# One SyncE queue, two weight loads moved behind two token-block transposes

## The chip, the cores and the metric

The kernel runs on one core of a Trainium2 chip. Its time is the device time of one execution in microseconds (us). Five engines work from instruction streams of their own: TensorE (PE, with its weight loads shown apart as PEld), VectorE (DVE), ScalarE (ACT), GpSimd (POOL) and SyncE (SP). SP computes nothing here: it issues every DMA of the kernel, in the order in which they stand in its stream. Three runs of the kernel before gave 298.45, 300.27 and 296.32 us, a median of 298.45 us.

## The reference

The program is one transformer block over 2048 tokens of width 640, in bf16. The first half normalises the tokens, projects them to Q, K and V, and runs attention of 32 heads of 20 channels in four segments of 512 tokens; each segment mixes a causal softmax attention of its own with a read from a memory that the segments before it have filled. The second half is a feed-forward layer of width 1728.

```python
for s in range(4):                       # segments of 512 tokens
    logits = einsum('bhqd,bhkd->bhqk', qs, ks) * scale + mask
    a_dot  = einsum('bhqk,bhkd->bhqd', softmax(logits), vs)
    num    = einsum('bhld,bhde->bhle', phi(qs), M)
    den    = einsum('bhld,bhd->bhl',  phi(qs), z)[..., None] + 1e-06
    outs.append(g * num / den + (1 - g) * a_dot)
    M = M + einsum('bhld,bhle->bhde', phi(ks), vs)
    z = z + phi(ks).sum(tokens)
h  = x + concat(outs) @ wo               # phi(t) = t+1 if t > 0 else exp(t)
h2 = h + silu(layernorm(h) @ w1) @ w2    # x is normalised before wq, wk, wv too
```

## The kernel before

Tokens are held in 16 blocks of 128. A segment is four blocks. For a segment the blocks are normalised (`layer_norm`: statistics on DVE, the reciprocal root on POOL, the subtraction and scaling on DVE into `xn_rot`, L772), and each normalised block is turned, so that channels lie on partitions, into a tile of `tT`. For blocks 0 to 3 TensorE does the turning; for all later ones SP issues a DMA transpose (L796). The name of that step is `n1_tr` and the block: `n1_tr8` to `n1_tr11` are the four blocks of segment 2. They read `xn_rot`, written by `n1_ap8` to `n1_ap11`.

TensorE then projects to Q and K (`pr`), V (`v`, from `wv_sb`), and works through the eight groups of four heads: scores (`qk`, L943), their exponentials on ACT (`e`, L964 or L960) with the causal mask on POOL (`mk`, L976), the product with V (`av`, L999), a turn back (`td`), and the division on DVE (`nm`). `mz` (L1117) adds a segment to the memory: 96 small matmuls for segment 0. The output of a segment goes through a transpose (`ot`, L1166), the output projection (`wo`, from `wo_sb`), a second normalisation, the feed-forward layer's first product (`h1`, from the five chunks of `w1_sb`), tanh and a multiply, and the second product (`h2`, from `w2_sb`). Work of one segment's attention is interleaved with the feed-forward work of the segment before.

What order the work has is written out by hand. One long list, `ORDER`, names every step, with the buffer slots that it takes and, behind a slash, its engine. A program walks over that list and appends each step to its engine's stream; waits on semaphores are put in where a step reads what another engine or a DMA writes. An engine does its steps strictly in list order, so a step that waits holds up all behind it on its engine.

The stretch of the list that the change touches lies in segment 1's attention. Weights that are used late are loaded there: `w_w1_0` to `w_w1_4` are five chunks of w1 (432 KB each), `w_wo` is all of Wo (800 KB), `w_w2_0` to `w_w2_5` are w2. They wait for the early weight loads to have been rearranged, which is long past here, and the first three chunks of w2 also wait for segment 0's Q and K, whose place they take. On SP the stretch reads, one after another: `w_w1_2`, `w_w2_0`, `kt04`, `n1_tr8`, `n1_tr11`, `w_w1_1`, `w_wo`, `n1_tr10`, `n1_tr9`, `w_w2_1`, `ot0`. The lines that record these are L586 (a weight load), L796 (a token transpose), L1106 (a transpose of the memory's keys, `kt`) and L1166 (`ot`).

Of the kernel before, what the change touches and what calls it, by code (L numbers as in the profile page):

```python
# [333 lines left out]
D = 640  # L334
# [54 lines left out]
mk6a mk6e mk6b qk7a0:4,2 e7a0:6 av5:6 e7a2 mk7a mz03:0 mz02 mz00 mz01 kt04:3 mz04 n1_tr8:1 ma0:0 n1_ap10:1 oe5/D:1  # L389
pr130.0:7 qk7b0:0,4 e7b0:0 e7b2 mk7b mzc1 pr130.1 qe130/D:0 pa130:0 v13.0:2 v13.1 ve13/D qk8a0:6,0 e8a0:1 td5:4 nm5:0  # L390
av6:5 oe6/D:0 pr140.0/C:2 e8a2 mk8a mb01:0 mzc0 mb00:0 ex101:0 av7:7 oe7/D:1 qk8b0:5,3 e8b0:6 e8b2 td6:0 nm6:3 pr140.1
qe140/D:0 td7:5 nm7:0 n1_tr11 w_w1_1 w_wo:0 n1_tr10 n1_tr9 qk8e0:6,0 e8e0:3 pr131.0:2 pa120:0 pr131.1 qe131/D pb101
pa131:0 e8e2 mzc4 mk8b mb02:0 qk9a0:6,3 e9a2:5 e9a0 pr121.0:5 pr121.1 qe121/D pa110:0 pr141.0:2 qk9b0:0,3 e9b0:0 e9b2
pr141.1/C qe141/D mk8e av8:5 oe8/D:0 w_w2_1 ot0:0 wo0.0/C:6 wo0.1/C rs0 n2_st0:2 n2_rs0 ex131:0 qk10a0:2,0 e10a0/W:2
ot1 wo1.0:4 wo1.1 rs1 n2_st1:7 ot2 wo2.0:6 ex120:1 qk10b0:0,2 e10b2/W:1 wo2.1 rs2 n2_ap0:1 pb120 ot3 wo3.0:4 wo3.1
# [932 lines left out]
```

## Time and profile before

| what | value |
|---|---|
| median of three runs, lowest, highest | 298.45, 296.32, 300.27 us |
| profiled execution, first to last instruction (the page gives its time as this span alone) | 298.8 us |
| PE busy | 282.4 us, 95% |
| DVE, ACT, POOL busy | 219.3, 216.6, 148.4 us |
| chain that ended last | PE 64%, ACT 16%, DVE 11%, issue 4%, DMA 2% |
| mean granted TensorE clock | 0.994 |

A row of a view of instructions in order of time gives the start, the time from the first to the last of the group's instructions, the engine, the source line, the operation, the tile written and the tiles read, and in brackets how long the engine had been idle and what ended that; "issue" means that the engine waited for nothing that the profile shows. A row of the view of stretches gives, for each engine, busy time and instruction count, then the granted clock, the busy share of the 16 DMA engines and the rate that they moved. In the view of DMA, queue q1 carries the transfers that SP issues; the two queues called "instruction" carry instructions to the engines.

### The profile page before, as it was taken

How to read it: one execution, taken by the hardware profiler on the slowest of the kernel's cores; microseconds unless marked ns; L12 is line 12 of the kernel's file. 1: busy time of each engine (PE TensorE's matmuls, PEld its weight loads, DVE VectorE, ACT ScalarE, POOL GpSimd, SP SyncE). 2: the span in 40 equal slices, each digit the busy share in tenths (PEclk: the TensorE clock that was granted, in tenths of full speed). 3: DMA queues.
4: the chain of work that ended last, by engine and by line, in shares of the span. 5: the costliest groups of instructions: out<-in, count | busy, mean ns of one | idle time of the engine just before them, and what ended most of it. 6: DMA issues, size and time to landing. Idle time of an engine off the chain costs nothing.

```text
span 298.8 us, 8471 instructions
## 1 busy us (share of the span) xinstructions
PE 282.4 (95%) x3537; PEld 158.5 (53%) x3561; DVE 219.3 (73%) x447; ACT 216.6 (72%) x263; POOL 148.4 (50%) x297
## 2 busy tenths in 40 slices
PE   7899889699999999999989899999999999999996
PEld 5554434345554454566643464466564557764574
DVE  4879899478999857889978958498664676733614
ACT  5899999589989999966889865979979741004500
POOL 4888786652787544955545652348554720300000
PEclk9999999989999999999999999999999999999999
DMA  7859359927430500353454321402331021320003
GB/s 223 283 183 201 54 126 220 207 75 114 82 77 1 121 2 3 57 104 59 47 134 123 63 48 29 80 2 40 75 68 46 2 53 39 66 76 14 0 2 110
DMA packets 48597, 24.72 MB, mean 83 GB/s; under 512 B 38896, under 2 KB 47472, under 8 KB 48560
## 3 DMA queue, kind: packets, MB, share of 16 engines
q1 hardware_dynamic: 48560, 24.19, 35.8%
q8 instruction: 28, 0.46, 0.7%
q14 instruction: 9, 0.07, 0.1%
HBM read 10.41 MB, written 2.62 MB: 44 GB/s over the span
## 4 chain that ended last, share of the span: by engine, by line
PE 64%; ACT 16%; DVE 11%; issue 4%; DMA 2%; POOL 2%; ACTq 0%; DVEq 0%
PE ps_all L550 46%; ACT PT L964 11%; PE ps_all L551 7%; PE ps_all L943 5%; PE ps_all L999 4%; DVE stt L754 3%; ACT PT L960 2%; DVE xn_rot L772 2%; DVE sT L1222 2%; DMA tT<-otok 2%; ACT th L1216 1%; POOL PT L976 1%; DVE x_tok L1181 1%; ACT ex L873 1%; PE ps_all L1117 1%
## 5 line engine op out<-in xcount | busy, mean ns | idle before, releaser
L964 ACT ACTIVATE PT<-ps_all 128x1024 bf16<-128x1024 f32 x114 | 109.3, 1035 | 18.9 <-PE ps_all L943 18.2
L976 POOL TENSOR_SCALAR_AFFINE_SELECT PT<-PT 128x512 bf16<-128x512 bf16 x128 | 82.0, 649 | 60.5 <-ACT PT L964 34.5
L1216 ACT ACTIVATE th<-ps_all 128x512 f32<-128x512 f32 (+1 forms) x56 | 31.6, 585 | 37.0 <-PE ps_all L550 28.1
L550 PE MATMUL ps_all<-w_sb,sT 128*128 128x320 bf16 x400 | 58.2, 299 | 0.1
L550 PE MATMUL ps_all<-tT,w_sb 128*128 128x512 bf16 x225 | 53.9, 379 | 1.7 <-DVE x_tok L1259 0.8
L1222 DVE SCALAR_TENSOR_TENSOR sT<-th,ps_all 128x512 bf16<-128x512 f32 (+1 forms) x56 | 36.2, 663 | 17.6 <-ACT th L1216 17.1
L550 PEld LDWEIGHTS ps_all<-w_sb,sT 128*128 128x128 bf16 x400 | 38.1, 98 | 16.6 <-issue 1.5
L960 ACT ACTIVATE PT<-ps_all 128x2048 bf16<-128x2048 f32 x23 | 43.2, 1879 | 3.4 <-PE ps_all L943 3.0
L550 PEld LDWEIGHTS ps_all<-tT,w_sb 128*128 128x128 bf16 x235 | 21.4, 98 | 25.4 <-issue 2.2
L754 DVE BATCH_NORM_STATS2 stt<-x_tok 128x6 f32<-128x320 bf16 x62 | 26.8, 474 | 1.2 <-DMA x_tok<-in_A_x_dram 1.1
L1259 DVE SCALAR_TENSOR_TENSOR x_tok<-ps_all,x_tok 128x640 bf16<-128x640 f32 (+1 forms) x17 | 13.2, 784 | 18.0 <-PE ps_all L550 17.1
L1077 POOL TENSOR_TENSOR otok<-on 128x320 bf16<-128x320 bf16 x24 | 19.2, 806 | 12.6 <-DVE on L1069 12.6
L867 DVE CAST QK<-ps_all 128x512 bf16<-128x512 f32 x26 | 17.9, 687 | 8.0 <-PE ps_all L550 6.5
L764 POOL TENSOR_TENSOR rst<-mvt,eps_c 128x1 f32<-128x1 f32 x32 | 7.0, 219 | 31.8 <-DVE mvt L757 30.0
L550 PE MATMUL ps_all<-tT,wkr 128*128 128x512 bf16 (+1 forms) x87 | 21.7, 368 | 0.7 <-issue 0.5
L550 PE MATMUL ps_all<-wv_sb,tT 128*128 128x320 bf16 x130 | 20.1, 303 | 2.3 <-issue 2.3
L550 PE MATMUL ps_all<-tT,wqr 128*128 128x512 bf16 (+1 forms) x79 | 20.0, 367 | 1.3 <-issue 0.6
L772 DVE TENSOR_SCALAR xn_rot<-x_tok,mvt,rst 128x640 bf16<-128x640 bf16 x32 | 17.8, 563 | 4.3 <-POOL rst L766 3.8
L1069 DVE TENSOR_TENSOR on<-ps_all,rd 128x640 bf16<-128x640 f32 x24 | 19.8, 824 | 0.8
L766 POOL TENSOR_TENSOR rst<-rst,eps_c 128x1 f32<-128x1 f32 x32 | 18.0, 563 | 2.5
L1015 DVE TENSOR_SCALAR oTs<-ps_all,lsc 128x512 bf16<-128x512 f32 x24 | 17.8, 742 | 1.7 <-PE ps_all L999 1.6
L999 PE MATMUL ps_all<-PT,Vx 128*32 128x512 bf16 (+3 forms) x384 | 17.3, 301 | 0.0
(113 smaller groups left out, 381.8 us busy)
## 6 DMA issues: line engine op xcount, KB each, us to landing
out_dram<-x_tok SPq DMA_DIRECT2D x15, 160.0 KB, 1.9
w_sb<-in_B_w_dram SPq DMA_DIRECT2D x5, 432.0 KB, 4.5
x_tok<-in_A_x_dram SPq DMA_DIRECT2D x3, 640.0 KB, 4.4
w_sb<-in_B_w_dram SPq DMA_DIRECT2D x3, 480.0 KB, 4.1
QKV<-QK SPq DMA_DIRECT2D x12, 72.0 KB
wv_sb<-in_A_wv_dram SPq DMA_DIRECT2D x1, 800.0 KB, 8.2
wo_sb<-in_A_wo_dram SPq DMA_DIRECT2D x1, 800.0 KB, 6.4
w_sb<-in_B_w_dram SPq DMA_DIRECT2D x1, 640.0 KB, 5.0
```

What stands on the lines that cost most here:

```text
L550: return [lambda e: e.matmul(out, lhsT=lhsT, rhs=rhs, start=start, stop=stop)]
L551: return [lambda e, p=p: e.matmul(out[p:p + 32, :], lhsT=lhsT[:, p:p + 32], rhs=rhs, start=start, stop=stop, tile_position=(0, p)) for p i ...
L754: T.add(DV, lambda e, hh=hh: e.bn_stats(out=stt[:, s, 6 * hh:6 * hh + 6], in_=xb[:, 320 * hh:320 * hh + 320]), reads=R((xa, xsub)), writes ...
L772: T.add(eng, lambda e: e.tensor_scalar(out=xn_rot[:, xn.slot, :], in0=x_tok[:, b % 12, :], scalar1=mvt[:, s, 0:1], scalar2=rst[:, s, :], o ...
L960: T.add(AC, lambda e: e.activation(out=o, in_=src, func=ACT.Exp, scale=SCALE), reads=[("ps", z.slot + q) for z in (a, b) for q in range(2) ...
L964: T.add(AC, lambda e: e.activation(out=pt[:, pta.slot, q0:q0 + 2, 0:width], in_=sc3[:, b0:b0 + 2, 0:width], func=ACT.Exp, scale=SCALE), re ...
L976: fns.append(lambda e, v=v: e.affine_select(out=v, in_=v, pattern=[[0, 4], [1, 128]], compare_op=ALU.is_ge, fill=0.0, base=0, channel_mult ...
L999: fns.append(lambda e, j=j, r=r, h=h, pa=pa, pt=pt, co=co, q0=q0, ji=ji: e.matmul(bank(po)[32 * r:32 * r + 32, q0:hi], lhsT=vtile(vx)[:, j ...
L1069: T.add(DV, lambda e: e.tensor_tensor(out=on[:, ona.slot, :, :].rearrange("p b (x e) -> p b x e", e=DH), in0=v[:, :, :, 0:DH], in1=r2.unsq ...
L1077: T.add(PO, lambda e: e.tensor_tensor(out=o_dst, in0=on[:, ona.slot, 0, :].rearrange("p (i x) -> p i x", i=4), in1=on[:, ona.slot, 1, :].r ...
L1216: T.add(AC, lambda e: e.activation(out=th[:, tha.slot, lo:hi], in_=bank(ps)[:, lo:hi], func=ACT.Tanh, scale=0.5), reads=R((ps, [0])), writ ...
L1222: T.add(DV, lambda e: e.scalar_tensor_tensor(out=sT[:, f, lo:hi], in0=th[:, tha.slot, lo:hi], scalar=1.0, in1=bank(ps)[:, lo:hi], op0=ALU. ...
```

## The change

Five names of the list are put in another order. `n1_tr9` and `n1_tr10` change places with each other and go in front of the loads of Wo and of w1's chunk 1, which change places with each other too.

```diff
-qe140/D:0 td7:5 nm7:0 n1_tr11 w_w1_1 w_wo:0 n1_tr10 n1_tr9 qk8e0:6,0 e8e0:3 pr131.0:2 pa120:0 pr131.1 qe131/D pb101
+qe140/D:0 td7:5 nm7:0 n1_tr11 n1_tr9 n1_tr10 w_wo:0 w_w1_1 qk8e0:6,0 e8e0:3 pr131.0:2 pa120:0 pr131.1 qe131/D pb101
```

All five are steps of SP. No instruction is added or removed, no other engine's stream changes its order, and every transfer has the size that it had.

## The prediction

> **What bounds the kernel now.** I began with the page: shares of the engines, the slices of time, the DMA queues, and the chain that ended last.
>
> ```profile
> span 298.8 us, 8471 instructions
> PE 282.4 (95%) x3537; PEld 158.5 (53%) x3561; DVE 219.3 (73%) x447; ACT 216.6 (72%) x263; POOL 148.4 (50%) x297
> q1 hardware_dynamic: 48560, 24.19, 35.8%
> q8 instruction: 28, 0.46, 0.7%
> PE 64%; ACT 16%; DVE 11%; issue 4%; DMA 2%; POOL 2%; ACTq 0%; DVEq 0%
> ```
>
> TensorE sets the end with nearly two thirds of the chain, and DMA waits are 2% of it. What deserves a look is the 4% of "issue", some 12 us in which the chain's engine waited for nothing visible. I went through the chain in order of time around the five moved steps, then took stretches there.
>
> ```profile
> core 0: us, PE busy (x) PEld busy (x) DVE busy (x) ACT busy (x) POOL busy (x), PEclk, DMA share, GB/s
> 50.60:55.84 5.24, 4.85 (x138) 2.48 (x137) 4.05 (x10) 4.86 (x6) 3.09 (x5) 1.00 0.91 275
> 55.84:58.17 2.33, 0.00 (x0) 0.00 (x0) 0.24 (x1) 0.64 (x1) 1.44 (x3) 1.00 1.10 103
> 58.17:62.20 4.03, 4.03 (x44) 1.79 (x48) 2.33 (x4) 2.35 (x3) 0.34 (x1) 0.58 0.55 147
> ```
>
> From 55.84 to 58.17 TensorE does nothing, the other engines run dry behind it, and afterwards the granted clock is 0.58 for 4.03 us. TensorE's own rows show that the hole lies inside one group of matmuls:
>
> ```profile
> 51.88 0.73 PE L999 MATMUL ps_all<-PT,sT 128*32 128x512 bf16 x16
> 52.47 0.94 PE L1117 MATMUL ps_all<-sT,phiKt 128*32 128x63 bf16 x96
> 54.86 0.98 PE L550 MATMUL ps_all<-wv_sb,tT 128*128 128x320 bf16 x6
> 58.17 1.08 PE L550 MATMUL ps_all<-wv_sb,tT 128*128 128x320 bf16 x4 [2.34 <-issue]
> 60.12 1.26 PE L999 MATMUL ps_all<-PT,sT 128*32 128x512 bf16 x16
> ```
>
> Ten matmuls of V's projection share operands that were there at 54.86; six run, four come 2.3 us late. No operand can be missing, so I looked for the instructions. Queue q8 moves 0.46 MB in 28 records, about 16.4 KB each, and PE and PEld have 3537 + 3561 = 7098 instructions: 253 to a record. So q8 is TensorE's instruction stream. Finding its records and counting what TensorE did between them gives:
>
> ```profile
> 31.90:42.75 10.85, 9.15 (x120) 4.52 (x120) 10.04 (x23) 10.85 (x13) 8.84 (x21) 1.00 0.40 92
> 42.75:55.70 12.95, 12.23 (x257) 5.86 (x256) 11.17 (x24) 12.49 (x15) 9.83 (x22) 1.00 0.83 228
> 42.75:51.75 9.00, 8.44 (x127) 3.62 (x125) 8.37 (x19) 8.93 (x11) 6.75 (x17) 1.00 0.78 191
> 55.70:61.05 5.35, 3.01 (x26) 1.20 (x28) 1.92 (x5) 1.97 (x3) 1.44 (x3) 0.75 0.89 151
> ```
>
> Records stood at 42.75, 55.70 and 61.05. Normally 240 instructions pass between two; here 513 passed, then 54. One block had been used up by about 51.75 (127 + 125 = 252), which is when the next was due; TensorE went on with the block that it still had, and that one is used up at 513: the stop. The 96 tiny matmuls at 52.47, with 96 weight loads, burn most of that block in one microsecond, so this block gives only 4.09 us of cover (51.75 to 55.84). What filled those 4 us on the DMA engines is SP's work:
>
> ```profile
> 47.93 2.62 SPq L796 DMA_TRANSPOSE tT<-xn_rot  x2
> 50.59 0.58 SPq L586 DMA_DIRECT2D w_sb<-in_B_w_dram  x1
> 51.21 0.43 SPq L586 DMA_DIRECT2D wo_sb<-in_A_wo_dram  x1
> 54.52 3.24 SPq L796 DMA_TRANSPOSE tT<-xn_rot  x2
> 57.81 0.58 SPq L586 DMA_DIRECT2D w_sb<-in_B_w_dram  x1
> 65.66 5.17 SPq L1166 DMA_TRANSPOSE sT<-otok  x4
> ```
>
> In half-microsecond stretches of the DMA view, q1 is full up to 55.5 and the instruction record comes in the next one:
>
> ```profile
> q1 hardware_dynamic: 154, 0.19, 104.7%
> q1 hardware_dynamic: 236, 0.11, 81.2%
> q8 instruction: 1, 0.02, 12.1%
> ```
>
> The first row is 55.0 to 55.5, the other two 55.5 to 56.0. The block was served when the queued w1 chunk and Wo were through. These are two of the loads that the change moves.
>
> **The change part by part.** It removes and adds nothing; only issue times and the traffic at 51.75 change. SP's order up to `n1_tr11` is the same, and so is all before 50.6 us.
>
> *The transposes.* Each waits for its normalised block:
>
> ```profile
> 50.77 0.43 DVE L772 TENSOR_SCALAR xn_rot<-x_tok,mvt,rst 128x640 bf16<-128x640 bf16 x1
> 53.83 0.66 DVE L772 TENSOR_SCALAR xn_rot<-x_tok,mvt,rst 128x640 bf16<-128x640 bf16 x1
> DMA to landing us min/median/max: 3.4/3.4/3.4
> 76.44 2.22 PE L550 MATMUL ps_all<-wv_sb,tT 128*128 128x320 bf16 x15
> ```
>
> `n1_tr9` can go at 51.20, when the first of these ends (0.6 us after SP is free), instead of about 55.8; `n1_tr10` at 54.5, as before. The landing row is `n1_tr9`'s of before: 55.8 + 3.4 = 59.2, and block 9 is read first at 76.44. It had 17 us to spare, so the earlier landing is worth nothing by itself.
>
> *The loads.* SP now stands at `n1_tr10` until 54.5, and behind that stand Wo and the w1 chunk. With 1.2 us of issue for the transpose (2.62 for two, above, is 1.3 each), Wo goes at about 55.8 instead of 51.2, the w1 chunk at 56.3 instead of 50.6, `w_w2_1` near 57 instead of 57.8.
>
> ```profile
> DMA to landing us min/median/max: 6.4/6.4/6.4
> 69.70 1.53 PE L551 MATMUL ps_all<-wo_sb,sT 128*32 128x320 bf16 x40
> L550 PE MATMUL ps_all<-tT,w_sb x25: 379/379/390, 88.4 to 97.7; 128*128 128x512 bf16 x25
> ```
>
> Wo took 6.4 us to land; from 55.8 that is 62.2, against 69.70 (or 66 with the hole gone). w1 is read from 88.4. Both are hidden; the cover is the 4 us between 62.2 and 66. The `ot` transposes, next on SP, wait for attention's output and are reached at about 62 then, not 65.66. Of the moved burst (800 + 432 + 480 KB with `w_w2_1`) 1712 KB are to be moved from about 57, and at 0.19 MB per half microsecond, the row above, that takes 4.5 us: through at 61.7. I charge nothing for it.
>
> *The instruction block.* Due at 51.75, it now finds one or two transposes in flight instead of 1232 KB of loads. Upper bound of the gain: the whole hole, 2.33, plus the slow clock. The clock's loss is at most 4.03 x (1 - 0.58) = 1.69; from single rows, the product with V took 1.26 against 0.73, so 0.53 is seen in that group alone. TensorE was busy 4.03 of 4.03 us there, so I take a value near the top, 1.5. Sum of the bounds: 0 to 4.0. Lower bound 0: the block comes as late as before. No trace row prices a block due between two transposes, so I bound its delay: with nothing in the way it would be under 1 us; with both transposes ahead of it, until about 53.6 to 54 (51.2 + 2.6, the issue time of two, as the scale). From record to first matmul it took 58.17 - 55.70 = 2.47 us, so a record by 53.4 leaves no hole and one at 54 leaves 0.6. I take 0.2 left.
>
> The engines all stood still together, so nothing had run ahead that could swallow the shift, and what follows hangs on TensorE's chain, not on fixed times. Sum: -2.33 - 1.5 + 0.2 = -3.6 us. Of the profiled 298.8 that leaves 295.2; the median of 298.45 stands 0.35 lower, so 294.9.
>
> [...]
>
> **The rivals.**
>
> *The loads are not what held the block (no change, 298.4).* TensorE may have stopped for something other than its instructions, the record may be late for its own reasons, or the DMA engines might serve q8 between q1's packets whatever is queued; then order in q1 is irrelevant and the hole stays. For: I infer the link from one coincidence in time and a second after 58, when the record of 61.05 also came at the end of a load. Against: both came just then, and 513 less 252 is one block. [...] The full q1 ahead of the record disagrees so far.
>
> *The hole only shrinks (about 296.7).* Transposes hold the block to about 54.5; the hole is 1.1 us, without the low clock or with half of it. Gain 1.2 from the hole and some 0.6 of clock: 1.8.
>
> *The hole moves (299.2, slower).* The next block is due when TensorE enters the last one, about 55.8, exactly where the moved burst now starts. Served first or between, it costs nothing. Served last, it decides by the end of the burst: the 114 + 119 instructions from 58.17 to 69.00 show that the block in hand lasts until about 65.4 once 3.6 us are gone. At the 7.0 us in which 1232 KB went before (50.6 to 51.2 + 6.4), 1712 KB take 9.7 us, to 65.5, and the first matmul 2.47 later: a hole of 2.6 us plus 1.7 of low clock, 4.3. The old gain of 3.6 is more than eaten: 299.2. At full rate, 61.7 + 2.47 = 64.2, just in time. It needs a record after 62.9.
>
> **How the numbers follow.** Forecast 0.60 (own range 293.3 to 296.3), no change 0.15, hole shrinks 0.13, hole moves 0.08; 0.04 for the rest. Runs of before spread from 296.32 to 300.27, about 2 us to either side. The range takes the forecast less 2.2 at the low end and, for the no-change case and the moved hole, 299.6 at the top. 2% is 6.0 us, about what a measurement of this kernel can tell from no change. No case gains that: it needs the 4.0 bound and a spread on top, 0.11. Slower by as much needs a moved hole and another of its size, 0.05. Within 2%: 0.84.
>
> **What would show it.** In the changed trace: the transposes on SP at about 51.2 and 54.5, Wo near 55.8; an instruction record between 52 and 54; 240 to 330 TensorE instructions since the one at 42.75, not 513; no "issue" gap inside V's projection, and clock 1.00 from 58 to 62. `ot` and the first use of Wo come 3 to 4 us earlier. A record still at 55 or later means that the transposes or nothing in q1 held it. A new gap at 65 to 66 means that the hole moved. If the hole is gone and the end has not moved, the shift was swallowed, which I have excluded.

## The result

| | before | changed |
|---|---|---|
| median of 20 runs | 300.0 us | 296.81 us |
| lowest to highest | 296.32 to 302.61 | 295.77 to 297.65 |
| span of the profiled execution | 298.8 us | 295.2 us |
| time of that execution | not given | 297.21 us |

The ratio is 0.992, with a 95% interval of 0.9894 to 0.9946: faster by 0.8%, far inside 2%. The comparison behind this ratio leaves out executions more than 1.5% above a kernel's fastest; before has such ones and the changed kernel has none, which is why the ratio is nearer to one than the medians (0.989).

The page of the changed kernel has nearly the same shares as before, in a span 3.6 us shorter:

```profile
span 295.2 us, 8471 instructions
PE 280.6 (95%) x3537; PEld 158.1 (54%) x3561; DVE 219.0 (74%) x447; ACT 216.5 (73%) x263; POOL 148.2 (50%) x297
PE 64%; ACT 17%; DVE 10%; issue 3%; DMA 2%; POOL 2%; ACTq 0%; DVEq 0%
```

The stretches of the hole, with the columns as before:

```profile
50.60:55.84 5.24, 4.85 (x139) 2.56 (x137) 4.09 (x9) 4.86 (x7) 3.09 (x5) 1.00 0.34 69
55.84:58.17 2.33, 1.64 (x22) 0.74 (x24) 1.09 (x3) 1.18 (x2) 1.40 (x3) 1.00 0.60 98
58.17:62.20 4.03, 3.39 (x70) 1.74 (x64) 3.65 (x10) 3.99 (x6) 1.99 (x6) 1.00 1.04 389
```

In the 5.24 us before the hole the DMA engines are busy at 0.34 instead of 0.91. TensorE now works in the stretch that was empty, and the clock behind it is 1.00 instead of 0.58. TensorE's and SP's rows in order of time:

```profile
52.62 0.94 PE L1117 MATMUL ps_all<-sT,phiKt 128*32 128x63 bf16 x96
56.69 0.72 PE L550 MATMUL ps_all<-wv_sb,tT 128*128 128x320 bf16 x4 [0.69 <-issue]
57.92 0.73 PE L999 MATMUL ps_all<-PT,sT 128*32 128x512 bf16 x16
66.70 1.53 PE L551 MATMUL ps_all<-wo_sb,sT 128*32 128x320 bf16 x40
48.09 7.80 SPq L796 DMA_TRANSPOSE tT<-xn_rot  x4
55.93 0.58 SPq L586 DMA_DIRECT2D wo_sb<-in_A_wo_dram  x1
56.55 1.00 SPq L586 DMA_DIRECT2D w_sb<-in_B_w_dram  x2
```

SP does what the order says, and Wo leaves at 55.93 (55.8 was worked out). The hole stands at the same place, ahead of the last four of the ten matmuls of V's projection, and is 0.69 us long instead of 2.34. The instruction record stands in the stretch from 54.0 to 54.5 (54.15 in a finer one), not at 55.7:

```profile
q8 instruction: 1, 0.02, 11.6%
```

Fewer instructions than before had been done when that record came, but not as few as was forecast: 240 matmuls and 240 weight loads since the record at 42.95, 480 together where 240 to 330 were expected.

```profile
42.95:54.15 11.20, 10.48 (x240) 5.05 (x240) 9.43 (x22) 11.12 (x13) 8.24 (x20) 1.00 0.68 166
```

The first use of Wo moved from 69.70 to 66.70, 3.0 us. The changed run was 0.15 us behind at the tiny matmuls (52.62 against 52.47), so 3.15 us were gained between the two: 1.65 in the hole, and the 1.5 that are left are the clock's. Another 0.6 us came between the first use of Wo and the end; from what is open.

### The profile page after: what moved, and what is told of

Same layout as the page of the kernel before. It is cut to its first block, busy times and chain, and to the rows that moved or that the text cites. A ratio compares the mean times of both kernels' runs of the same rounds, so it can differ in the third digit from the quotient of the medians.

```text
span 295.2 us, 8471 instructions
## 1 busy us (share of the span) xinstructions
PE 280.6 (95%) x3537; PEld 158.1 (54%) x3561; DVE 219.0 (74%) x447; ACT 216.5 (73%) x263; POOL 148.2 (50%) x297
## 3 DMA queue, kind: packets, MB, share of 16 engines
HBM read 10.41 MB, written 2.62 MB: 44 GB/s over the span
## 4 chain that ended last, share of the span: by engine, by line
PE 64%; ACT 17%; DVE 10%; issue 3%; DMA 2%; POOL 2%; ACTq 0%; DVEq 0%
PE ps_all L550 47%; ACT PT L964 12%; PE ps_all L551 7%; PE ps_all L943 5%; PE ps_all L999 4%; DVE stt L754 3%; ACT PT L960 2%; DVE xn_rot L772 2%; DVE sT L1222 2%; DMA tT<-otok 2%; ACT th L1216 1%; ACT ex L873 1%; POOL PT L976 1%; DVE x_tok L1181 1%; PE ps_all L1117 1%
```

## Is it an instruction block that makes the hole?

Two kernels move the boundaries of TensorE's instruction blocks and leave all DMA orders as in the kernel before. In `fills_plus10` ten dummy matmuls are added at the start:

```diff
-n1_rs0 vpad0 n1_ap0:1 fill25:3 n1_tp0:5 n1_te0:2 fill5:2 re_wq0/A:0
+n1_rs0 vpad0 n1_ap0:1 fill25:3 n1_tp0:5 n1_te0:2 fill15:2 re_wq0/A:0
```

> The order of DMA is that of the kernel before. Ten more dummy warm-up matmuls at 7.6 us (20 instructions with their weight loads) move every block boundary of TensorE's stream 20 instructions forward. Theory: the block is due near 50.2 us, before the two loads are in the queue, so its record comes at 50.5 to 52 us and there is no hole in V's projection although Wo and w1 stand where they stood; gain 3.9 us less about 1 us of dummy work: 2 to 3 us under before. Rival (the loads delay something else than the instructions): hole of 2.3 us at the same matmul, time 1 us above before.

Measured: 299.92 us median (296.27 to 303.56), ratio 0.9982 (0.9925 to 1.0039). The expected gain did not come, but the hole moved. TensorE in order of time, and below it TensorE's instructions up to a moment inside the hole (PE and PEld counts), for this kernel, for the one before and for the changed one:

```profile
54.80 0.39 PE L943 MATMUL ps_all<-QKV 20*128 20x384 bf16 x6
57.26 0.23 PE L943 MATMUL ps_all<-QKV 20*128 20x128 bf16 x2 [2.07 <-issue]
```

```profile
0.00:56.50 56.50, 49.11 (x593) 26.41 (x598) 45.16 (x108) 49.55 (x66) 42.24 (x113) 1.00 0.71 191
```

```profile
0.00:57.00 57.00, 49.53 (x593) 26.00 (x598) 45.47 (x110) 51.59 (x68) 42.76 (x114) 1.00 0.73 192
```

```profile
0.00:56.40 56.40, 49.34 (x593) 25.92 (x598) 45.29 (x110) 51.31 (x68) 42.09 (x113) 1.00 0.65 175
```

All three stop after 593 matmuls and 598 weight loads (in the other kernels that stop, 593 to 598 matmuls are counted, but always 598 weight loads; the page lists 3537 matmuls to 3561 weight loads, so some matmul records seem to be missing). With ten more matmuls in front, that count falls ten matmuls earlier in the program: two scores, two of Q's projection and six of V's. The hole follows the count, not the operation, its operands or its buffers. That is what an absent block of instructions would do, and a late operand or buffer would not. What failed in the expectation is that the block would be due early enough to slip in ahead of the loads: the record came at 54.6.

`fills_minus10` leaves out ten of the 25 dummies (`fill25:3` becomes `fill15:3`).

> The DMA order is that of before; ten of the 25 dummy matmuls at the start are left out, so that every block boundary of TensorE lies 20 instructions later in the program. Theory: the hole moves from the middle of V's projection to behind it, to the scores or the turn back that follow (8 + 8 + 4 instructions further), some 0.9 us later in time; the record comes only 0.3 us later, as the boundary before the tiny matmuls is crossed 0.3 us later; hole 1.4 to 1.8 us instead of 2.3, and the median 1 to 2 us under before. Rival (the hole is tied to V's projection or its operands): same matmul, same hole.

Measured: 297.4 us median (295.18 to 302.14), ratio 0.9925 (0.9876 to 0.9974). In the profiled execution there is no hole at all; all ten matmuls of V run in one piece:

```profile
56.72 1.52 PE L550 MATMUL ps_all<-wv_sb,tT 128*128 128x320 bf16 x10
```

Its start was slower: from 10.5 to 13.9 us the granted clock was 0.50 here and 1.00 in the kernel before, and this execution was 1.85 us behind at the tiny matmuls. The reason isn't shown: the profiled execution of `after_minus10`, with the same dummies, had no such stretch. The missing hole is no proof that the boundary's place alone removes it either. SP issued Wo at 53.75 here, 2.5 us later than before, and the record came in the quarter of a microsecond from 54.25, when no packet of Wo had moved (those of 2 to 8 KB are the w1 chunk's, Wo's are smaller than 2 KB: in the kernel before, all 10 from 52.00 to 52.25 are of the first kind, all 152 from 54.5 to 55.0 of the second):

```profile
DMA packets 11, 0.05 MB, mean 204 GB/s; under 512 B 0, under 2 KB 0, under 8 KB 10
q8 instruction: 1, 0.02, 27.8%
```

So it was tried once more with as many dummy columns as before. `before_wide15` has 15 dummies of 427 columns, 6405 in all, in place of 25 of 256, 6400:

```diff
-    zpad = sb("zpad", [128, 256], BF16)
+    zpad = sb("zpad", [128, 427], BF16)
-        PE, [lambda e: e.matmul(bank(a)[:, 0:256], lhsT=zpad[:, 0:128], rhs=zpad[:, :], start=True, stop=True)] * n,
+        PE, [lambda e, w=427 if n > 5 else 256: e.matmul(bank(a)[:, 0:w], lhsT=zpad[:, 0:128], rhs=zpad[:, 0:w], start=True, stop=True)] * n,
-fill25:3
+fill15:3
```

> DMA order of before; 15 dummy matmuls of 427 columns at the start in place of 25 of 256, so that TensorE is warmed for as long as before but every block boundary lies 20 instructions later in the program. Theory (a late instruction block makes the hole, and whether it is late depends on where the boundary lies as well as on the loads): as in the look with ten dummies fewer, no stop at instruction 1191 and a clock of 1.00 in most runs, median 2 to 3.5 us under before, with the two loads where they were. Rival (the earlier look without a hole was one lucky run, the loads in front are enough to make the hole): hole of 1.5 us or more after 1191 counted instructions, some 20 instructions later in the program, and a median within 1 us of before.

Measured: 297.09 us median (295.47 to 299.75) beside 300.03 for the kernel before on the same chip; the ratio of 0.997 (0.9918 to 1.0022) doesn't settle it. The profiled execution has a hole:

```profile
56.39 0.21 PE L550 MATMUL ps_all<-ident,oTs 128*128 128x84 bf16 x1
58.16 0.28 PE L550 MATMUL ps_all<-ident,oTs 128*128 128x84 bf16 x3 [1.56 <-issue]
```

It lies nine or ten matmuls later in the program than before's, inside the turn back, which is the place expected of `fills_minus10`, and again behind 598 weight loads:

```profile
0.00:57.00 57.00, 50.34 (x597) 24.96 (x598) 45.75 (x111) 52.04 (x69) 43.06 (x115) 1.00 0.76 192
```

So the count holds with the boundary moved either way. The hole is 1.56 us long with the loads where they were: the "no stop" was wrong, and the rival's hole was there. It is shorter than the 2.34 us of before because it begins later, not because the block came sooner: the record stands at 55.9 (55.7 before) and the next matmul at 58.16 (58.17 before). The median of all runs is 2.9 us lower without any load being moved, and 2 of the 12 have a mean clock of 0.994 or lower, against 13 of before's 23; with an interval that holds 1, this is a hint. `fills_minus10`, whose interval doesn't hold 1, shows that ten dummies fewer are worth time, by the boundary's place or by what else they shift.

## Which of the moved steps counts?

`swap_only` exchanges Wo with the w1 chunk and `n1_tr9` with `n1_tr10`, but keeps the loads in front:

```diff
-n1_tr11 w_w1_1 w_wo:0 n1_tr10 n1_tr9
+n1_tr11 w_wo:0 w_w1_1 n1_tr9 n1_tr10
```

> The changed pairs are exchanged among themselves (Wo before the w1 chunk, n1_tr9 before n1_tr10), but the two loads stay in front of the two transposes. Theory (the instruction block of TensorE waits for the loads queued in front of it): the same 1232 KB stand in front, so the record stays near 55.7 us, the hole in V's projection stays at 2.0 to 2.7 us with a low clock behind it, and the time stays at that of before, ratio 0.995 to 1.005. Rival (the order within each pair, or n1_tr9 landing early, was worth the gain): hole under 1 us and a ratio near 0.99.

Measured: 300.93 us median (297.54 to 303.0), ratio 1.0031 (0.9979 to 1.0083). The order within the pairs is worth nothing that these runs can tell. The hole was longer than expected, 3.45 us, with the record at 56.1, in an execution of 302.24 us, among the longest of the ten.

`wo_behind` moves only Wo, `w1_behind` only the w1 chunk:

```diff
-n1_tr11 w_w1_1 w_wo:0 n1_tr10 n1_tr9
+n1_tr11 w_w1_1 n1_tr9 n1_tr10 w_wo:0
```

```diff
-n1_tr11 w_w1_1 w_wo:0 n1_tr10 n1_tr9
+n1_tr11 w_wo:0 n1_tr9 n1_tr10 w_w1_1
```

> Wo behind both transposes, the w1 chunk still in front of them (432 KB in front of the instruction block instead of 1232). Theory as it stands after the first runs (with nothing queued the block's record comes near 54, which leaves a hole of 0.3 to 0.7 us; the loads add about 2 us): record near 54.3 to 55, hole 0.5 to 1.4 us, mean clock 1.00 in most runs, median 0.5 to 1 us above the changed kernel's. Rival (Wo alone, as the longer load, is the whole effect): record and hole as in the changed kernel. Rival (any one load in front delays the block fully): record near 55.7, hole 2.3 us.

> The w1 chunk behind both transposes, Wo still in front of them (800 KB in front). Theory: between the kernel before and the one with only the w1 chunk in front: record 54.5 to 55.5, hole 0.8 to 1.9 us. Rival (the w1 chunk is the whole effect): record and hole as in the changed kernel. Rival (any one load delays it fully): hole 2.3 us.

Measured: `wo_behind` 297.39 us median (296.77 to 297.94), ratio 0.9926 (0.9891 to 0.9962), record at 54.0. `w1_behind`: 300.6 us median (297.54 to 301.96), ratio 1.0012 (0.9966 to 1.0059), record at 55.9. TensorE's rows, first of `wo_behind`, then of `w1_behind`:

```profile
56.36 0.72 PE L550 MATMUL ps_all<-wv_sb,tT 128*128 128x320 bf16 x4 [0.42 <-issue]
```

```profile
58.48 0.72 PE L550 MATMUL ps_all<-wv_sb,tT 128*128 128x320 bf16 x4 [2.62 <-issue]
```

As far as these ratios tell, Wo is the whole effect. The 432 KB of w1 in front cost nothing, against the expectation. In `wo_behind` all but 12 of their packets had gone by 53.5, and the record came at 54.0, about where it stands with no load in front at all (54.15 in the changed kernel). Whether Wo counts for its size, for its rows or only because it is still running at that time was not tried apart.

`more_ahead` puts a third load, 480 KB of w2, in front as well:

```diff
-n1_tr11 w_w1_1 w_wo:0 n1_tr10 n1_tr9
+n1_tr11 w_w1_1 w_wo:0 w_w2_1 n1_tr10 n1_tr9
-mk8e av8:5 oe8/D:0 w_w2_1 ot0:0
+mk8e av8:5 oe8/D:0 ot0:0
```

> The kernel before with the load of another w2 piece (480 KB) moved up behind Wo, also in front of the two transposes: 1712 KB in the queue instead of 1232. Theory: at 0.19 MB per half microsecond the record comes 1.3 us later, near 57.0, and the hole grows from 2.3 to 3.6 us; span 1.3 us or more above that of before. Rival (the DMA engines take turns between queues, and the record was late for its own reasons): record near 55.7, hole 2.3 us, time as before.

Measured: 301.07 us median (296.91 to 302.62), ratio 0.999 (0.9922 to 1.0057), record at 56.4, hole 2.89 us. The record came 0.7 us later than before, not 1.3 (in `swap_only`, with no more in front than before, it came 0.4 later), and while q1 was still full:

```profile
q1 hardware_dynamic: 157, 0.20, 106.2%
q1 hardware_dynamic: 157, 0.18, 99.6%
```

These are 56.0 to 56.5 and 56.5 to 57.0. In `fills_plus10` too the record, at 54.6, stands in the middle of the loads. So the block didn't simply wait for all that was queued, nor did it pass it: in before, `before_wide15`, `swap_only`, `w1_behind` and `more_ahead` it stood at 55.7 to 56.4, against 54.0 to 54.3 with Wo behind (and the boundary where it was), 1.4 to 2.4 us later, and the 480 KB more made no measurable difference to the time.

## What is left with nothing in the way?

`tr10_first` has both loads behind, as the changed kernel, but `n1_tr10` first, so that SP issues nothing until 54.5 us:

```diff
-n1_tr11 w_w1_1 w_wo:0 n1_tr10 n1_tr9
+n1_tr11 n1_tr10 n1_tr9 w_wo:0 w_w1_1
```

> Both loads behind both transposes, as in the changed kernel, but n1_tr10 before n1_tr9; SP then stands until 54.5 us before it issues anything. Theory: at 51.75 us only the tail of n1_tr11 is in flight, the record comes at 52 to 52.7 us, no hole is left in V's projection (0 to 0.1 us, against 0.69 in the changed kernel), span 0.7 us under the changed kernel's. Rival (a block takes some 2.4 us from its due time whatever is queued): record near 54.2 and a hole near 0.7 us again.

Measured: 297.12 us median (296.39 to 298.19), ratio 0.9931 (0.9895 to 0.9966). The DMA view of this kernel, first for 52.00 to 54.30, then for the half microsecond behind it, and TensorE's row:

```profile
DMA packets 8, 0.00 MB, mean 0 GB/s; under 512 B 8, under 2 KB 8, under 8 KB 8
q1 hardware_dynamic: 8, 0.00, 0.3%
```

```profile
q8 instruction: 1, 0.02, 13.5%
```

```profile
56.74 0.72 PE L550 MATMUL ps_all<-wv_sb,tT 128*128 128x320 bf16 x4 [0.33 <-issue]
```

With the DMA engines idle for 2.3 us the record still came at 54.3, and a hole of 0.33 us was left. It is shorter than the changed kernel's 0.69 because this execution reached the place 0.42 us later (V's projection starts at 55.44, against 55.02), not because the block came sooner. The rival was right on the record: a good part of the block's lateness has nothing to do with q1. From record to the next matmul it took 2.4 us here, 2.5 in the kernels before and after, 2.6 in `w1_behind` and `fills_plus10`.

With Wo behind, that lateness changes with the boundary's place. `after_minus10` is the changed kernel with `fill15:3` for `fill25:3`, `after_wide15` the changed kernel with the wide dummies shown above.

> The changed kernel with ten of the 25 dummy matmuls left out. Theory: the block in hand lasts 0.9 us longer in time and the refill starts 0.3 us later, so the hole of 0.69 us becomes 0 to 0.2, and the median is 0.3 to 0.7 us under the changed kernel's 296.8, if the start is not slower without the dummies. Rival (the boundary's place does not matter): hole 0.7 us in V's projection as before.

> The changed kernel with 15 dummy matmuls of 427 columns in place of 25 of 256. Theory: no hole, no run with a lower clock, median 295.5 to 296.2, that is 0.6 to 1.3 us under the changed kernel's 296.8 and 1.3 to 1.6% under before. Rival (fewer dummies gain or lose at the start of the kernel, not at the boundary): first projection later or earlier than 10.1 us by as much as the median moves, and the hole of 0.7 us in V's projection still there.

Measured: `after_minus10` 295.8 us in four runs (295.13 to 298.15), ratio 0.9891 (0.9813 to 0.9969), record at 52.5. `after_wide15` 295.98 us median of 12 (295.26 to 296.74), ratio 0.9955 (0.992 to 0.999) beside a kernel before with a median of 300.03; record between 53.5 and 53.75. Neither has a hole there; `after_wide15`:

```profile
54.91 1.52 PE L550 MATMUL ps_all<-wv_sb,tT 128*128 128x320 bf16 x10
10.09 0.71 PE L550 MATMUL ps_all<-tT,wqr 128*128 128x256 bf16 x5
```

The first projection starts at 10.09 us, as in the kernel before, so the start gave nothing. All 12 runs lie under 296.75. The median is 0.8 us under the changed kernel's, about the 0.69 us of the hole that was left. The two were not timed side by side; the medians of the kernel before that stand beside them agree (300.03 and 300.0), but the two ratios, 0.9955 and 0.992, would rank them the other way. By its median it is the fastest version here with more than four runs.

## Why the prediction was right or wrong

**The bound and the cause: right.** The hole is a missing block of TensorE instructions. The count of 1191 in three kernels, and of 598 weight loads in all that stop, shows it better than the prediction's own argument did.

**"The block was served when the queued w1 chunk and Wo were through": half right.** Wo decided (record at 55.9 with Wo alone in front), the w1 chunk did not (54.0 with the chunk alone).

**"One block had been used up by about 51.75 ... which is when the next was due": not as put.** In `tr10_first` nothing was in the way after 52.0 and the record came 2.3 us later, 2.0 after the count of 930 at which the prediction has the block due (52.3 there). "With nothing in the way it would be under 1 us" was guessed too low. Counted the same way, the record was 4 us late in the kernel before and is 2.25 us late in the changed one, so the loads had made some 1.7 of the 4 us; the prediction took nearly all of it for theirs. This is why 480 instructions and not 240 to 330 were done at the record, and why 0.33 to 0.69 us of hole stay where 0.2 was taken. The rest of the sentence, 2.47 us from record to matmul and "one at 54 leaves 0.6", held: 54.15 left 0.69.

**The slow clock at 1.5 us: right.** 1.5 is what the hole doesn't explain, and no run of the changed kernel had a mean clock under 0.999.

**Swallowed or not: right.** 3.0 us of 3.6 were there at the first use of Wo, and none was lost behind it. The rivals of a moved hole and of no change did not come: between 61 and 67 us, where the next boundary lies, TensorE's one wait is the 0.58 us for `otok` ahead of 61.45, which before has too, ahead of 64.45. The time of "the hole only shrinks", 296.7, did come, by luck: its hole of 1.1 us, held open by the transposes, didn't, and `tr10_first` shows the same lateness without them.

**The last step failed: "Of the profiled 298.8 that leaves 295.2; the median of 298.45 stands 0.35 lower, so 294.9."** The span became 295.2, as worked out, with some luck: the hole gave 1.65 us where 2.13 were counted, and the 0.6 us behind the first use of Wo, which stand in no term, made up for it. But a span isn't a time: the changed kernel's profiled execution took 297.21 us for its 295.2, 2.0 more. By the same 2.0 the profiled execution of before took about 300.8 us, and was not close to the median of three but 2.3 us above it. The gain of that one slower execution was taken off a median that need not hold it; whether the hole of those three runs was shorter isn't on record, as none of them has a trace. From 300.8 the same sum gives 297.2. Of the 1.9 us between the forecast 294.9 and the measured 296.81, some 1.55 are the base: the median of 20 runs of before is 300.0, not 298.45. The rest is the size of the gain in a typical run: 3.2 us between medians of 20, or 0.8% and 2.4 us by the ratio, against 3.6. Measured, 296.81 lies outside the forecast's own 293.3 to 296.3 and inside the whole range.

The spread of before's three runs, 4 us, should have said that something in them varied. In the 31 executions of before beside `swap_only`, 18 have a mean clock of 0.994 or lower, which is what one stretch of low clock leaves (0.58 over 4.03 us takes 1.7 of 298.8 us); the changed kernel's 20 have none. Whether the block came later in those 18 than in the other 13, and why, no trace shows.

## What to carry to other kernels

When an engine stops inside a group of instructions whose operands are all there, count its instructions up to the stop in two versions of the kernel; if the count is the same, look for the record of its instruction block and for what SP queued in front of it, and try the kernel with the long loads behind it. Here, with the boundary where it was, the record stood at 55.7 to 56.4 with the 800 KB of Wo in front and at 54.0 to 54.3 with Wo behind; the 432 KB of w1 alone did not delay it (54.0). A few instructions more or less, far ahead, moved the boundary and changed the stop too: ten dummies fewer took the changed kernel's from 0.69 us to none. Take a sum made on one profiled span off the time of that execution, and treat a stall in it as one draw of a spread when the runs differ by more than the gain.

## What was not expected of the hardware

In one trace of each kernel, TensorE's stops of 0.33 to 1.56 us at this place had no lower clock behind them (1.00 in the 4 us behind the 0.69 of the changed kernel); those of 2.07 us and more did: 0.66 in the 4 us behind the 2.07 of `fills_plus10`, 0.58 behind 2.34, 0.57 behind 2.89, 0.50 behind 3.45. First the 4 us behind the stop of 1.56 us in `before_wide15`, then those behind the 2.62 us in `w1_behind` (the clock is the number third from the end):

```profile
58.16:62.16 4.00, 3.41 (x68) 1.79 (x68) 3.19 (x7) 2.23 (x4) 1.94 (x5) 1.00 0.53 140
```

```profile
58.48:62.48 4.00, 4.00 (x48) 2.01 (x52) 2.23 (x4) 2.45 (x3) 0.89 (x2) 0.69 0.52 194
```

The shortest of these stops with a lower clock behind it took 2.07 us. The clock was nearly half of the 3.15 us that the change gained up to the first use of Wo, 1.5.

With the DMA engines idle from 52.0 us in `tr10_first`, the record of TensorE's block stood at 54.3, and 2.4 us more went by to the next matmul; with Wo in front, the record stood 1.4 us and more later (54.6 in `fills_plus10`, whose boundary lies 20 instructions earlier; 2.2 to 2.6 us from record to matmul again, 3.0 in `swap_only`). Why its record is at 54.3 with idle DMA engines, why Wo delays it and the w1 chunk doesn't, and what the boundary's place does to it are open.
